# Another order and another choice of engines for the 4663 steps of a transformer block on one core

## The chip, the core and the metric

The kernel runs on one core of a Trainium2 chip. A core has five instruction streams that run side by side: TensorE (PE) for matrix products, VectorE (DVE), ScalarE (ACT) and GpSimd (POOL) for elementwise work, and SyncE (SP), which here issues every DMA. Each stream is executed strictly in order; streams wait for each other, and for DMAs, through semaphores. Products land in PSUM, which POOL cannot read; everything else lies in SBUF or in DRAM. The metric is the device time of one execution in microseconds; the number given is the median of several runs.

## The reference

One pre-norm transformer block over 2048 tokens with 512 channels, in float32:

```
h   = x + attention(layernorm(x)) @ wo         # 32 heads of 16, causal, window of 256
out = h + (sigmoid(n @ w_gate) * (n @ w_up)) @ w_down,   n = layernorm(h)     # F = 1376
```

Attention masks every key that is in the future or 256 or more positions back, takes a softmax over the rest and weighs the values with it.

## The kernel before

**Numbers in halves.** Apart from the product with v, every float32 operand of a product is split into a float16 high half and a float16 low half, and a product is three matmuls: high x high, high x low, low x high (`mm3`, the loop in `multiply`). Making the halves costs two elementwise steps: a copy or scaling to float16 (ACT or DVE: L355, L357, L954, L1024, L1104) and a subtraction (DVE or POOL: L362, or DVE alone where a scale is applied: L956, L1026).

**Stages.** First x is normalized (`do_ln`), and wq, wk, wv are loaded, scaled and split (`prep`). For each of 8 blocks of 256 tokens the kernel then makes q and k (`do_qk`), v (`do_v`), the scores once for their row maximum (`do_s`: PE L740, DVE L725), feeds the maxima back as extra rows of the queries by DMAs (`do_m`), makes the scores again, transposed (`do_st`: L794 to L805), takes their exponentials (ACT L770), zeroes the masked corners (POOL L778, L783), multiplies with v (`do_pv`: L831), transposes the result by a DMA and adds the halves (`do_o`: L861), divides by the sums (`do_wo`: L875), splits (L362), transposes (to `oT`) and multiplies with wo, adding x (L899).

The GLU stage works on pairs of 128-token tiles. `do_ln2` normalizes the pair, splits it (L1104, L362) and transposes it by a DMA; the buffer of halves, `hl2`, is one deep, so the second half of a pair's work on ACT waits for the first transposition. `do_pair` multiplies with the gate and up weights by a scheme of seven products in place of eight (P1 to P7, L1140); the sums between them are elementwise steps on DVE or ACT (`copied`, `added`). `gated` takes the sigmoid (ACT L1206) and the product of gate and up (L1210); `hidden` forms the sums S1 to S4 (L1224) and splits four rows (L355 or L357 for the high half, L362 for the low), each then transposed by a DMA (L1240). `do_down` multiplies with w_down (L1317, L1323), again by seven products, and adds to h (L1288, L1300). The weights are prepared beside the attention and at the start of the GLU stage: w_gate and w_up by `do_weights` (subtractions T1 to T4: L1045 and L362), w_down by `do_split` (subtractions D1 to D4: L362; halves L954, L956).

**What sets the order.** The kernel is written as 492 pieces, each one or more Python generators. A generator yields before a step with the engines that may take it, the events it needs and the ring buffers it takes. A list of numbers, `ORDER`, says which generator runs its next step and on which engine; `Planner.run` walks the list once and emits the instructions of each step. So the list fixes, for each of the five streams, which instructions it gets and in what order. One number holds three things:

```
self.now = self.roots[code >> 7]                # the piece of work
item = self.now[code >> 2 & 31]                 # its part
self.on = next(iter(costs)) if len(costs) == 1 else ENGINES[1 + (code & 3)]   # 0 DVE, 1 ACT, 2 POOL
```

Steps with a choice of engine call `alt(...)`: the copies `cp`, `hhi`, `hi`, `raw`, `v`, `qk` (ACT or DVE), the subtractions and sums `lo`, `lo2`, `less`, `less2`, `dless`, `hsum`, `hlo`, `gate`, `oadd`, `on`, `wlo` (POOL or DVE), the maxima `am`, `amax` (ACT or DVE). The costs written beside them were used by the search that made the list and play no part when the kernel runs; the position in the list is not a time, only an order.

Of the kernel before, what the change touches and what calls it, by code (L numbers as in the profile page):

```python
# [61 lines left out]
    3203, 3331, 771, 899, 1027, 1155, 7424, 2179, 2435, 7808, 7426, 1411, 7424, 641, 2051, 7810, 7424, 641, 1539, 7424, 1667, 7808, 641, 7427, 7808,  # L62
    3459, 7810, 1795, 641, 2307, 6658, 640, 7424, 3587, 643, 7811, 640, 2691, 3075, 641, 7808, 2947, 640, 641, 2819, 640, 641, 8323, 640, 641, 8323,
    640, 8323, 1280, 1281, 1921, 8323, 1921, 3715, 8195, 1281, 1280, 1920, 8323, 13056, 1921, 8323, 8323, 8323, 1280, 12672, 13058, 1283, 8321, 8195,
    8195, 1280, 8195, 3843, 12674, 8195, 2561, 8195, 1920, 7042, 8320, 8195, 8195, 1281, 1923, 8193, 1280, 8451, 2561, 2560, 8192, 1281, 1280, 1281,
    8579, 9219, 1280, 1281, 2561, 3971, 8451, 9219, 1280, 8451, 8835, 12672, 8579, 6018, 1920, 8835, 12673, 8451, 13056, 9219, 1921, 8451, 12672,
    8451, 4099, 1921, 8451, 18304, 8451, 8963, 8579, 1922, 8449, 8579, 8963, 2560, 8579, 1921, 8448, 8579, 8835, 6274, 8579, 1921, 13056, 8579, 8963,
    17920, 12675, 13058, 8577, 2563, 12673, 8576, 17922, 1920, 1921, 8707, 13059, 18306, 7683, 8707, 1920, 13057, 1920, 7683, 1921, 8067, 1920, 8067,
    1920, 7683, 17920, 49667, 8067, 23168, 17921, 4227, 8067, 17920, 8707, 7683, 50691, 8064, 7681, 51075, 2560, 9091, 17923, 18304, 13443, 8707,
    2561, 13443, 23552, 13443, 2561, 13443, 17921, 13443, 18304, 4355, 23554, 13443, 18304, 13443, 6402, 9091, 13443, 28416, 13571, 13441, 13571,  # L70
    6530, 9091, 13571, 10371, 10371, 13571, 10372, 10376, 6786, 13571, 13440, 13571, 13571, 13571, 10371, 10371, 10371, 13569, 10384, 23170, 13699,
    10388, 13699, 50688, 2562, 13699, 10380, 49665, 13699, 13568, 13699, 13699, 13699, 13699, 23168, 10371, 10371, 14467, 10371, 13697, 13827, 10392,
    10400, 13827, 4483, 9347, 10396, 13827, 9348, 14211, 13827, 13696, 9347, 9347, 9347, 13827, 14083, 9352, 13827, 9360, 10883, 14211, 9356, 13827,
    10884, 13827, 28800, 14211, 18307, 13825, 10883, 9347, 10883, 18305, 9364, 10888, 13824, 9347, 10883, 2561, 9368, 18691, 13955, 10892, 33664,
    18691, 2561, 14083, 9347, 18691, 23169, 18691, 14467, 9372, 9347, 18691, 10896, 23170, 13955, 18819, 9376, 9603, 18691, 14467, 9604, 10883, 10883,
    9603, 10900, 18691, 10904, 51203, 9608, 18691, 23552, 10883, 9603, 9603, 18689, 18819, 10908, 4611, 9616, 18819, 10883, 9612, 18819, 10912, 18819,
    18688, 18819, 18819, 13955, 9603, 9603, 18819, 9603, 50435, 2560, 2561, 18817, 18947, 51331, 18947, 9620, 9624, 14339, 18947, 9628, 51073, 18947,
    18816, 14083, 9603, 18947, 2561, 18947, 14339, 18947, 2562, 18947, 50179, 9632, 11139, 10115, 19075, 18945, 10116, 10115, 11140, 19075, 10120,
    13955, 2561, 6146, 11139, 11139, 19075, 11144, 11148, 19075, 2561, 18944, 11139, 7170, 10115, 19075, 10115, 11152, 19075, 10128, 19075, 14339,
    10124, 11139, 12931, 11156, 34048, 28418, 11139, 10115, 10115, 19075, 12931, 19073, 10136, 11160, 12931, 10132, 51201, 19072, 11139, 11139, 10115,  # L80
    12931, 11164, 11168, 10140, 10115, 13315, 12929, 10144, 50433, 12416, 11651, 11651, 11651, 13315, 11652, 11656, 12419, 11660, 11651, 13315, 11664,
    11907, 11907, 13315, 11908, 11912, 0, 11651, 11651, 11651, 18563, 13313, 11668, 11672, 12419, 11676, 51329, 11651, 11907, 11907, 11680, 23171,
    11916, 18563, 49411, 11920, 23169, 23552, 19203, 11907, 11907, 11907, 18563, 11928, 23554, 19203, 11924, 11932, 11907, 16387, 16387, 11936, 9475,
    9475, 18563, 33666, 16388, 9477, 9481, 16392, 16387, 28802, 16387, 18561, 9475, 16396, 16387, 9475, 6914, 9485, 12544, 16387, 9489, 23555, 16400,
    12547, 16404, 9475, 23553, 16387, 18179, 16408, 28416, 16387, 9497, 15619, 16412, 9475, 4739, 18179, 16416, 50177, 50051, 15620, 15619, 9731,
    24195, 9501, 12547, 15624, 15619, 15619, 24195, 9733, 15628, 28417, 15619, 9731, 15632, 9731, 24195, 19203, 9741, 15636, 15619, 24195, 9737,
    15640, 15619, 15619, 9731, 15644, 9731, 9745, 24195, 15648, 9753, 15363, 9750, 9731, 15364, 15363, 24195, 9757, 19331, 9506, 15368, 10243, 16899,
    15363, 24195, 10245, 16900, 9494, 10243, 10243, 15372, 9859, 16899, 10249, 16899, 9762, 24195, 10253, 38912, 50049, 15363, 10243, 28418, 10243,
    9859, 10257, 16908, 10265, 16904, 7298, 49409, 15376, 16899, 28800, 10243, 15363, 16912, 16899, 10269, 10499, 4867, 18179, 15380, 50819, 9857,
    16916, 10499, 10274, 15363, 18179, 19331, 10501, 15384, 10505, 9856, 10499, 15363, 18177, 16899, 14851, 10499, 15388, 10509, 24323, 28419, 10513,  # L90
    16920, 10499, 14852, 10518, 15363, 10499, 10521, 16899, 15392, 24323, 10262, 50563, 16924, 10525, 14851, 16899, 24323, 14856, 19331, 50817, 14851,
    11011, 16928, 10530, 24323, 19459, 11013, 14851, 14860, 24323, 39296, 11011, 10627, 14851, 19459, 11011, 14851, 10627, 11021, 28801, 49795, 14872,
    19459, 11017, 14864, 28802, 24193, 14868, 11011, 9987, 11011, 11025, 14851, 24192, 24323, 11033, 2562, 11011, 14876, 14851, 14595, 11037, 28803,
    11267, 14880, 24323, 14595, 11030, 14596, 11269, 11267, 14595, 10625, 14600, 11267, 24323, 34050, 11273, 14604, 14595, 14595, 11277, 11042, 14608,
    11267, 11281, 11267, 14612, 14595, 11289, 11267, 11286, 14616, 14595, 11395, 14595, 19587, 10624, 11293, 11779, 17155, 14620, 11781, 10755, 11779,
    11298, 14624, 11785, 11779, 17155, 24321, 17664, 17155, 11395, 17156, 11789, 17667, 49793, 24320, 17160, 11779, 17164, 17155, 24451, 11779, 11793,
    17168, 19843, 24451, 11801, 11779, 11798, 19844, 17155, 19843, 11805, 17172, 12035, 17155, 17667, 19848, 12037, 12035, 11810, 19843, 17176, 12041,
    12035, 17155, 19852, 12045, 19587, 12035, 17155, 17180, 12049, 12035, 19843, 11393, 17184, 12035, 12054, 19843, 19856, 12061, 19715, 19843, 19860,
    19843, 12057, 29443, 19715, 11392, 12163, 20867, 29443, 19864, 19715, 12066, 29443, 14723, 19587, 19843, 33664, 14723, 14725, 12163, 19868, 51843,
    33665, 19872, 4995, 14729, 20868, 20867, 50561, 14723, 20872, 20867, 14723, 14733, 29443, 20876, 20867, 14737, 20867, 29443, 20880, 14723, 12161,  # L100
    20884, 20867, 14742, 14723, 14749, 20867, 24067, 20892, 20867, 14753, 24067, 20888, 14979, 24067, 12160, 14981, 14758, 24067, 20896, 14979, 9986,
    16131, 24067, 44160, 14985, 14979, 14746, 16131, 11523, 29443, 14989, 14979, 16132, 16131, 29443, 16136, 14993, 14979, 16140, 16131, 16131, 15005,
    24067, 14998, 16144, 14979, 16148, 16131, 16131, 15009, 15491, 16152, 29443, 15002, 16156, 15493, 20099, 24067, 15014, 20100, 15491, 20099, 15491,
    10754, 20104, 20099, 16131, 24067, 16160, 20099, 12291, 15107, 15107, 24065, 29440, 20108, 17792, 15501, 20112, 17795, 15497, 29440, 51840, 20099,
    15105, 15491, 49539, 20116, 15491, 20099, 15505, 23939, 20120, 23939, 15517, 17795, 12288, 15491, 20099, 11520, 20611, 15521, 20611, 15747, 15514,
    20612, 23939, 49923, 15749, 20124, 15747, 15510, 23939, 20616, 15753, 20099, 15747, 20128, 20611, 20611, 15757, 15526, 15747, 20620, 23939, 15761,
    15104, 20611, 15747, 23939, 20624, 15773, 15747, 15770, 20611, 20628, 23939, 19203, 15777, 15766, 7552, 20611, 16259, 24064, 20611, 15875, 16259,
# [1392 lines left out]
```

## Time and profile before

| what | value |
| --- | --- |
| median of 3 runs | 767.21 us (766.03 to 768.69) |
| the profiled execution | span 769.3 us; the profile gives no other time for it |
| TensorE matmuls | 729.6 us busy, 95% |
| VectorE | 692.9 us, 90% |
| ScalarE | 436.9 us, 57% |
| GpSimd | 256.7 us, 33% |
| DMA, the queue of all transfers | 117.35 MB, 67.9% of 16 engines' span |

"Busy" is the union of an engine's instruction spans. A group row names line, engine, operation, output<-inputs, shapes and count, then the group's busy time in us, the mean of one in ns, and the idle time of the engine just before its instructions with what ended it. In a timeline row the first two numbers are start and length in us; a bracket at the end gives the idle time before the row and its releaser. Attention runs until about 460 us, with the first GLU products mixed in from 415 on; from there to the end it is the GLU stage.

### The profile page before, as it was taken

Reading aid. Unit: us, or ns where it says so; the run is one execution under the profiler, and the core shown is the slowest. Engines: PE = TensorE matmul, PEld = TensorE weight load, DVE = VectorE, ACT = ScalarE, POOL = GpSimd, SP = SyncE. Lnnn points to the kernel's source line nnn. Section 1 sums busy time; section 2 is a strip of 40 time slices with the busy share of each in tenths; the row PEclk is TensorE's granted clock in tenths of the full one; section 3 lists DMA queues with packets and bytes.
Section 4 is the critical chain, followed back from the end, with each engine's and each line's share of the span. In section 5 each row is a group of like instructions: output and inputs, shape, how many; then the busy total and the mean of one; then the engine's idle time right before and its main releaser. Section 6 shows DMA issues by size and latency. Waiting matters only on the chain.

```text
span 769.3 us, 19057 instructions
## 1 busy us (share of the span) xinstructions
PE 729.6 (95%) x7030; PEld 502.0 (65%) x7030; DVE 692.9 (90%) x2067; ACT 436.9 (57%) x774; POOL 256.7 (33%) x319
## 2 busy tenths in 40 slices
PE   4899999999999999999999898699999999999997
PEld 3586678777686687686666554367565666666476
DVE  8999999978899999999998579999998989989973
ACT  5755788878688888798877667653222111121210
POOL 3333445535545466554757442240000000000000
PEclk9999999999999999999999999899999999999999
DMA  8586593886747989569587879455375665736535
GB/s 300 156 221 168 142 180 80 152 198 144 165 95 172 205 211 182 166 156 245 150 162 180 211 187 274 117 119 105 79 136 95 117 131 106 150 66 109 96 83 155
DMA packets 210318, 118.57 MB, mean 154 GB/s; under 512 B 174576, under 2 KB 183792, under 8 KB 210224
## 3 DMA queue, kind: packets, MB, share of 16 engines
q1 hardware_dynamic: 210224, 117.35, 67.9%
q8 instruction: 55, 0.90, 0.5%
q14 instruction: 39, 0.32, 0.2%
HBM read 43.65 MB, written 19.40 MB: 82 GB/s over the span
## 4 chain that ended last, share of the span: by engine, by line
PE 75%; DVE 11%; DMA 5%; issue 5%; ACT 3%; SPq 0%; DVEq 0%; ACTq 0%
PE mmp L402 18%; PE sp L1140 14%; PE mmp L1317 11%; PE pvp L831 7%; PE sp L740 6%; PE stp L1140 6%; PE pvp L1140 3%; PE stp L805 2%; PE stp L795 2%; DVE junk L725 2%; PE stp L794 1%; PE mmp L1323 1%; PE stp L796 1%; DMA oT<-whl 1%; ACT pa L770 1%
## 5 line engine op out<-in xcount | busy, mean ns | idle before, releaser
L725 DVE CUSTOM_DVE_ANT_0 junk<-sp,mask 128x320 uint8<-128x320 f32 (+4 forms) x512 | 215.4, 465 | 16.6 <-PE sp L740 14.0
L770 ACT ACTIVATE pa<-stp,kappa 128x512 f32<-128x512 f32 (+1 forms) x256 | 157.3, 645 | 48.0 <-PE stp L796 44.5
L1140 PEld LDWEIGHTS <-x 128*128 128x128 f16 x1008 | 98.3, 98 | 94.6 <-issue 10.1
L740 PE MATMUL sp<-SK,SQ 96*128 96x256 f16 (+3 forms) x960 | 129.6, 233 | 6.3 <-DVE mq L725 3.1
L402 PE MATMUL mmp<-xT,W 128*128 128x256 f16 x768 | 114.3, 281 | 3.3 <-DVE sq L661 1.7
L740 PEld LDWEIGHTS <-SQ 96*128 96x128 f16 x960 | 80.5, 97 | 30.9 <-issue 12.8
L1140 PE MATMUL sp<-W,x 128*128 128x512 f16 (+1 forms) x420 | 90.1, 351 | 6.5 <-ACT SQ L355 5.8
L770 ACT ACTIVATE pb<-stp,kappa 128x512 f32<-128x512 f32 x128 | 84.6, 685 | 19.7 <-PE stp L805 15.9
L402 PEld LDWEIGHTS <-W 128*128 128x128 f16 x768 | 71.4, 100 | 16.1 <-DVE W L539 2.9
L778 POOL TENSOR_SCALAR_AFFINE_SELECT pa<-pa 128x1024 f32<-128x1024 f32 x56 | 62.9, 1127 | 53.9 <-ACT pa L770 50.3
L831 PE MATMUL pvp<-pa,VT 128*17 128x128 f32 (+1 forms) x1408 | 62.5, 307 | 0.0
L795 PE MATMUL stp<-SQ,SK 100*128 100x256 f16 x224 | 60.2, 272 | 0.0
L563 POOL TENSOR_TENSOR rs<-rs,nhalf 128x1 f32<-128x1 f32 x32 | 20.2, 634 | 118.2 <-DVE rs L560 105.0
L783 POOL TENSOR_SCALAR_AFFINE_SELECT pa<-pa 128x512 f32<-128x512 f32 x64 | 42.6, 669 | 45.3 <-ACT pa L770 45.0
L1206 ACT ACTIVATE SQ<-sp,cg 128x512 f32<-128x512 f32 (+1 forms) x22 | 14.0, 636 | 76.6 <-PE sp L1140 76.3
L796 PE MATMUL stp<-SQ,SK 100*128 100x128 f16 x256 | 55.5, 219 | 0.7 <-ACT pb L770 0.4
L783 POOL TENSOR_SCALAR_AFFINE_SELECT pb<-pb 128x512 f32<-128x512 f32 x64 | 42.0, 658 | 42.6 <-ACT pb L770 40.1
L402 PE MATMUL mmp<-WO,oT 128*128 128x512 f16 x192 | 51.4, 389 | 2.5 <-DMA oT<-whl 2.5
L831 PEld LDWEIGHTS pvp<-pa,VT 128*17 128x17 f32 x1408 | 37.8, 97 | 22.7 <-issue 2.7
L362 DVE TENSOR_TENSOR SQ<-SQ,SQ 128x512 f16<-128x512 f32 (+3 forms) x93 | 50.2, 555 | 1.9 <-ACT SQ L355 1.3
L794 PE MATMUL stp<-SQ,SK 100*128 100x128 f16 x224 | 49.5, 221 | 1.3 <-DMA SQ<-mt 0.3
L805 PE MATMUL stp<-SQ,SK 100*128 100x256 f16 x256 | 48.1, 272 | 2.5 <-ACT pa L770 2.1
(226 smaller groups left out, 1445.8 us busy)
## 6 DMA issues: line engine op xcount, KB each, us to landing
SQ<-sq SPq DMA_DIRECT2D x96, 128.0 KB
wr<-chunk SPq DMA_DIRECT2D x28, 256.0 KB
SK<-mem SPq DMA_DIRECT2D x16, 384.0 KB
chunk<-in_wd_dram SPq DMA_DIRECT2D x20, 256.0 KB
X<-in_x_dram SPq DMA_DIRECT2D x16, 256.0 KB
mem<-sk SPq DMA_DIRECT2D x8, 512.0 KB
out_dram<-X SPq DMA_DIRECT2D x16, 256.0 KB
W<-wr SPq DMA_DIRECT2D x7, 512.0 KB
```

What stands on the lines that cost most here:

```text
L402: PE.matmul(ps, a_of(a, k), b_of(b, k), start=(k == 0 and i == 0), stop=(k == n - 1 and i == 2))
L725: V.tensor_tensor_reduce(out=junk[:, c0:], in0=ps[:, c0:], in1=mask[:, c0:], scale=1.0, scalar=-3.0e38, op0=ALU.add, op1=ALU.max, accum_ou ...
L740: PE.matmul(ps[:, col:col + k1 - k0], q, SK[0:96, (2 * a + hf) % 5, 4 * (p % 2) + j, k0:k1], start=True, stop=True)
L770: S.activation(dst, a, AF.Exp, scale=kappa)
L778: G.affine_select(out=f, in_=f, pattern=[[0, 8], [-1, 128]], compare_op=ALU.is_gt, fill=0.0, base=0, channel_multiplier=1)
L783: G.affine_select(out=p, in_=p, pattern=[[0, 4], [1, 128]], compare_op=ALU.is_ge, fill=0.0, base=0, channel_multiplier=-1)
L795: PE.matmul(a[:, 128:384], ks(k0 + 1, g, j), qs(b, g, j, 0, 256), start=True, stop=True)
L796: PE.matmul(a[:, 384:512], ks(k0 + 3, g, j), qs(b, g, j, 128, 256), start=True, stop=True)
L805: PE.matmul(a[:, u, :], ks(k0 + 2, g, j + u), qs(b, g, j + u, 0, 256), start=True, stop=True)
L831: PE.matmul(ps[32 * j:32 * j + 17, u, q0:q1], VT[:, kt % 6, 8 * j + g, :], w[:, j, c:c + q1 - q0], start=first, stop=last, skip_group_chec ...
L1140: PE.matmul(ps, X2[p % 2][part][:, (a * COUNT[part] + at) * 2 + k, :], operand(c, j)[:, b, k, :], start=first and k == 0 and i == 0, stop= ...
L1317: PE.matmul(ps, hT[p, c, r][:, a, half * kinds[c] + i, :], W["d"][2 * c + i][:, b, j, :], start=fresh and c == 0 and i == 0 and n == 0, st ...
```

## The change

Only the list `ORDER` is replaced. The new one has 4663 entries like the old: every step of every generator is there once, so the matmuls, the transfers and the arithmetic are the same. What differs is the order within each stream and the engine of steps that have a choice. In words the change is described as: order and engine of all steps searched anew over the whole kernel, with transfers that land late by varying amounts and a shared port of VectorE and GpSimd.

```diff
 ORDER = [
-    3203, 3331, 771, 899, 1027, 1155, 7424, 2179, 2435, 7808, 7426, 1411, 7424, 641, 2051, 7810, 7424, 641, 1539, 7424, 1667, 7808, 641, 7427, 7808,
...
-    61591, 62224, 62211, 62211, 62211, 62211, 62228, 62211, 62231, 62211, 62211, 62211, 62232, 62235,
+    3203, 7427, 7427, 3331, 3587, 7811, 7811, 7427, 7043, 13059, 13059, 771, 7425, 1027, 899, 643, 1155, 643, 7811, 7424, 1539, 2179, 7808, 2051,
...
+    62211, 62146, 62211, 62211, 62147, 62227, 62211, 62211, 62211, 62211, 62211, 62211, 62231, 62231, 61591, 62211, 62235, 62235,
 ]
```

Two entries show how it reads. The gate product of pair 0, chunk 1 is entry 57500 in the old list (piece 449, part 7, engine 0: DVE) and 57502 in the new (engine 2: POOL). The sum S1 of the same pair is 57512 and becomes 57514. By kind, the steps that change from DVE to POOL are 48 sums S1 to S4, 21 gate products, 42 low halves of rows, the subtractions of `do_split`, `do_weights` and `do_ln2`, and 11 additions of `do_o`; from DVE to ACT go mostly the copies `cp` (30) and high halves `hhi` (39).

| engine | steps before | steps after | in the old mutual order |
| --- | --- | --- | --- |
| TensorE | 1729 | 1729 | 1081 |
| VectorE | 1424 | 1217 | 524 |
| ScalarE | 710 | 767 | 479 |
| GpSimd | 299 | 449 | 175 |
| SyncE (DMA) | 501 | 501 | 249 |

The last column is the largest number of steps that stand on the engine in both lists and in the same order.

438 rows, old and new, of the table ORDER are left out of this document.

## The prediction, made before the result

> **What bounds the kernel now.** I read the page first, then the busy time by stretch, then the instructions around each pause of TensorE, then the groups by shape.
>
> ```profile
> span 769.3 us, 19057 instructions
> PE 729.6 (95%) x7030; PEld 502.0 (65%) x7030; DVE 692.9 (90%) x2067; ACT 436.9 (57%) x774; POOL 256.7 (33%) x319
> ...
> DVE  8999999978899999999998579999998989989973
> ...
> POOL 3333445535545466554757442240000000000000
> ```
>
> TensorE (PE) and VectorE (DVE) are both near full, but these are averages over different stages. GpSimd (POOL) stops working after slice 23. The stretches, cut where the stages change:
>
> ```profile
> core 0: us, PE busy (x) PEld busy (x) DVE busy (x) ACT busy (x) POOL busy (x), PEclk, DMA share, GB/s
> 0.00:40.00 40.00, 26.87 (x176) 17.68 (x177) 35.45 (x84) 25.92 (x51) 13.22 (x28) 0.96 0.73 230
> 40.00:415.00 375.00, 365.61 (x4486) 272.69 (x4484) 351.62 (x1318) 293.85 (x517) 195.22 (x236) 1.00 0.75 168
> 415.00:460.00 45.00, 42.86 (x455) 24.07 (x454) 28.71 (x58) 31.56 (x52) 22.30 (x26) 1.00 0.79 193
> 460.00:505.00 45.00, 34.90 (x173) 17.09 (x172) 44.41 (x88) 31.36 (x58) 9.81 (x10) 0.89 0.80 202
> 505.00:760.00 255.00, 254.74 (x1708) 166.81 (x1708) 230.77 (x520) 54.26 (x99) 16.17 (x22) 1.00 0.56 107
> 760.00:769.00 9.00, 4.59 (x41) 3.63 (x38) 1.99 (x3) 0.00 (x0) 0.00 (x0) 0.99 0.41 148
> ```
>
> Read the first number after each length: PE is idle for 13.1, 9.4, 2.1, 10.1, 0.3 and 4.4 us, 39.4 in all. From 505 to 760, a third of the span, it does not pause. That "busy" is real there: six matmuls of 512 columns start 1.30 us before the next six, then 1.29, with nothing in between, and one wait of 0.6 us stands in the whole stretch.
>
> ```profile
> 639.94 1.46 PE L1140 MATMUL sp<-SK,x 128*128 128x512 f16 x6
> 641.24 1.46 PE L1140 MATMUL stp<-SK,x 128*128 128x512 f16 x6
> ```
>
> ```profile
> PE sp L1140 <- ACT SQ L355: 0.6, 1, 0.6
> ```
>
> So whatever the new lists do after 505, they can only lose there; a gain must come from before. The narrowest place is 460 to 505, where DVE works 44.41 of 45 us while PE rests for 10.1. PE's largest pauses from 415 on:
>
> ```profile
> 432.41 0.38 PE L805 MATMUL stp<-SQ,SK 100*128 100x256 f16 x2 [1.94 <-ACT pa L770]
> ...
> 464.07 4.36 PE L402 MATMUL mmp<-WO,oT 128*128 128x512 f16 x12 [2.14 <-DMA oT<-whl]
> ...
> 485.84 0.91 PE L1140 MATMUL stp<-W,x 128*128 128x352 f16 x5 [1.13 <-DVE W L1026]
> ...
> 495.61 1.92 PE L1140 MATMUL sp<-W,x 128*128 128x352 f16 x6 [5.77 <-ACT SQ L355]
> ```
>
> The last is the costliest. ScalarE's (ACT's) queue just before it, then POOL's and DVE's:
>
> ```profile
> 492.87 0.72 ACT L954 ACTIVATE WD<-chunk,sd 128x512 f16<-128x512 f32 x1 [2.25 <-POOL chunk L362]
> 494.57 0.63 ACT L355 ACTIVATE SQ<-SQ 128x512 f16<-128x512 f32 x1 [0.99 <-DVE SQ L1210]
> 495.11 0.45 ACT L355 ACTIVATE SQ<-sp 128x352 f32<-128x352 f32 x1
> ```
>
> ```profile
> 475.04 2.15 POOL L362 TENSOR_TENSOR chunk<-chunk 128x256 f32<-128x256 f32 x1 [6.04 <-DVE WD L956]
> ...
> 491.89 0.94 POOL L362 TENSOR_TENSOR chunk<-chunk 128x256 f32<-128x256 f32 x1 [6.48 <-DVE chunk L362]
> ```
>
> ```profile
> 491.34 0.41 DVE L362 TENSOR_TENSOR chunk<-chunk 128x256 f32<-128x256 f32 x1
> ...
> 493.85 1.29 DVE L1210 TENSOR_TENSOR SQ<-SQ 128x512 f32<-128x512 f32 x2
> ```
>
> PE waits for a PSUM copy (495.11) that is ready to run but stands in ACT's queue behind a half of a w_down piece (492.87). That half waits for a POOL subtraction, which waits for a DVE subtraction (491.34 + 0.41) inside a DVE queue without a gap. A full DVE reaches PE by way of two other queues.
>
> **The change part by part.** Nothing is added or removed: both lists hold the same 4663 steps, hence the same matmuls and transfers. I followed both lists through the planner's loop and counted, for each step, its engine and its place on that engine. In all 170 go from DVE to POOL and 20 back, 98 from DVE to ACT and 41 back. The prices:
>
> ```profile
> L362 DVE TENSOR_TENSOR chunk<-chunk 128x256 f32<-128x256 f32 x12 | 4.9, 413 | 0.0
> L362 POOL TENSOR_TENSOR chunk<-chunk 128x256 f32<-128x256 f32 x8 | 8.5, 1057 | 32.3 <-DVE chunk L362 17.2 <-DVE WD L956 11.5 <-ACT WD L954 2.3
> L1224 DVE TENSOR_TENSOR SQ<-SQ 128x256 f32<-128x256 f32 x62 | 26.7, 437 | 0.5
> L1224 POOL TENSOR_TENSOR SQ<-SQ 128x256 f32<-128x256 f32 x2 | 1.6, 784 | 2.9 <-DVE SQ L1224 2.9
> L362 DVE TENSOR_TENSOR SQ<-SQ,SQ 128x512 f16<-128x512 f32 x46 | 31.0, 683 | 0.9 <-ACT SQ L355 0.7
> L875 POOL TENSOR_TENSOR OS<-OS,rc 128x512 f32<-128x512 f32 x9 | 9.9, 1102 | 4.0 <-DVE rc L873 4.0
> L861 DVE TENSOR_TENSOR OS<-RT 128x272 f32<-128x272 f16 x17 | 8.5, 511 | 0.0
> L861 POOL TENSOR_TENSOR OS<-RT 128x272 f32<-128x272 f16 x15 | 11.4, 763 | 4.2 <-DVE whl L362 4.2
> L362 DVE TENSOR_TENSOR whl<-OS,whl 128x512 f16<-128x512 f32 x9 | 6.6, 735 | 0.0
> L362 DVE TENSOR_TENSOR X<-X 128x512 f32<-128x512 f32 x3 | 3.0, 986 | 0.0
> ```
>
> *460 to 505.* Of the steps that stand in this stretch now, 27 leave DVE for POOL: 8 subtractions of do_split, 3 of do_weights, 6 sums and 3 gates of the GLU, 5 low halves of rows, a normalization and a split of do_wo. One low half comes back, and 3 high halves come from ACT. DVE loses 8 x 0.413 + 11 x 0.437 (256 and 352 columns) + 8 x 0.683 (512 columns) = 13.6 us and gets back 0.683 + 3 x 0.437 = 2.0: its 44.4 become 32.8. POOL gets 11 x 1.057 + 8 x 0.784 + 8 x 1.102 = 26.7, less 1.1 for the one that leaves: its 9.8 become 35.4. PE is busy for 34.9. Three engines then stand near 35 where one stood at 44.4, so the ceiling of the gain is PE's idle 10.1. Against it: the subtractions D1, D3, D2, D4 of w_down now all run on POOL, in one queue with the sums, and 17 POOL steps stand from the sum S1 of the first pair to the last D4, on which a half in ACT's queue waits, with a PSUM copy of pair (0, 2) behind it. PE has over the same steps 5 groups of six 512-column matmuls (1.30 us each by the spacing above), 5 of six with 352 columns (352/512 of that) and 8 of three (half): 16.2 us. At 1.0 us per POOL step the copy comes about in time, at 1.2 us it is 17 x 1.2 - 16.2 = 4.2 us late. Ends: -10 and +5. I take -4, nearer to PE's idle row, since the ACT copy still stands behind such a half.
>
> *40 to 415.* 28 steps go from DVE to POOL (11 of L861, 5 splits of do_wo, 3 subtractions of do_weights, 2 normalizations, the rest small) and 12 come back (4 normalizations, 4 splits of do_ln, 2 splits of do_wo, 2 of L861). The large ones: 9 x 0.511 + 3 x 0.735 + 3 x 0.986 = 9.8 us off DVE, less 2 x 0.683 + 4 x 0.683 = 4.1 back; the small rest (8 steps near 0.43) gives 3.4: 9.1 net, of 351.6. Between DVE and ACT 21 go one way and 22 the other, taken as nothing. DVE is idle for 23.4 us here and so not the bound all the time; PE shows 9.4 idle. Ends: -9 (all of it reaches PE) and +4 (PE's local order changes too, only 1081 of its 1729 steps keep their mutual order, and nine of the old gaps of 0.4 us would make 4). I take -2, a quarter of the relief.
>
> *0 to 40.* 13 steps leave DVE, 8 come to it, at the same order of prices; PE's first work stays in place. Ends -2 and +1; -0.5.
>
> *The transfers.* Only 249 of the 501 DMA steps keep their mutual order on SyncE's (SP's) queue, so loads of the w_gate and w_up halves and the transpositions to oT, mt and x2 pass each other. What a late one costs now is seen twice above: 2.14 (oT), and 1.94 behind the second half of ln2, which ACT starts only when hl2's first transposition has landed:
>
> ```profile
> 423.87 6.67 DMA x<-hl
> ```
>
> In the new lists the first half (L1104) stands 3.3 us of PE work earlier, with the matmuls around it in the old order; the oT transposition of the same place has the same kind of neighbours. SP itself waits, head of the queue:
>
> ```profile
> SPq L752 <- DVE mq L725: 33.4, 9, 6.7
> ```
>
> and whatever is queued behind waits with it. Ends: -4 (both pauses gone) and +6.7 (one more such wait reaches PE whole). I take -1.
>
> *505 to 760.* 111 steps go to POOL, 68 to ACT, 15 come to DVE. At the cheap end, 0.437 each, DVE sheds 164 x 0.437 = 72 us: 230.8 become 159. Nothing to win under a PE without a pause; each row chain (gate, two sums, low half) gets longer by 0.42 + 2 x 0.35 + 0.42 = 1.5 us, which two buffers of pairs in flight cover. If that cover goes, the next matmul of a pair waits. Ends 0 and +10; +1.
>
> *End.* The last 38 PE steps are the same in both. The last low half goes to POOL (1.1 against 0.68); the transposition that PE now waits for is behind it: 0, ends -1 and +2.
>
> Sum against the profiled execution: 769.3 - 4 - 2 - 0.5 - 1 + 1 = 762.8. Its span is the only time that execution has, 2.1 above the median of the three timed runs (767.2); I carry that over: **761**.
>
> Here a rule speaks against the change. POOL's same subtraction took 2.15 us at 475.04 and 0.94 at 491.89, in a stretch where DVE never rests. The Trainium skill, SBUF — State Buffer, "Who interferes with whom", says that a DVE instruction with two SBUF inputs and a GpSimd instruction that reads SBUF exclude each other: the later one blocks in full. The trace agrees in kind, 1.2 us lost once. It makes the third rival below, which is priced from rows.
>
> **The rivals.** *POOL takes DVE's place (slower).* Between 460 and 505 POOL's mean rises from 1.0 toward 2.15 because DVE's two-input work alternates with it. From 45 / (27 + 10) = 1.2 us per instruction POOL needs more than the whole stretch; at 1.5 it needs 55, 10 us more than now, with ACT's halves and copies behind it: 769.3 + 10 - 3.5 (other terms but GLU) - 2.1 = about 774. For it: the 2.15 and the row's mean of 1.057. Against: 0.94 beside a full DVE, and DVE is emptier afterwards.
>
> *Nothing measurable.* The 4 of 460 to 505 are lost to POOL's queue and a moved transfer takes 2 more: 769.3 - 2 - 0.5 + 2 - 2.1 = 766.7. For it: three quarters of the changes lie after 505, where PE is the bound. Against: DVE's 44.4 of 45 is relieved for sure.
>
> *The port in the GLU stage (slower).* Were every POOL instruction there to block DVE for its length, 111 x 1.057 = 117 us come on DVE's 159: 276 of 255, and PE waits: 761 + 21 = 782. It decides only if more than (255 - 159) / 117 = four in five block. Unlikely.
>
> *All of it.* The 10 of PE's idle, the 9 of DVE's relief and the 4 of transfers come whole: 769.3 - 23 - 2.1 = 744.
>
> **How the numbers follow.** Forecast (757 to 764.8) 0.47, all of it 0.09, nothing 0.18, POOL in DVE's place 0.22, the port 0.04. About 0.3%, 2.3 us, can be told from no change. Faster 0.56, same 0.18, slower 0.26. The low end takes half of the way to "all of it", 749; the high end the POOL rival with a moved transfer, 777. The forecast's own range is 755 to 766.
>
> **What would show it.** Right: DVE near 33 to 36 and PE idle under 7 in the 45 us before PE's pauses end; POOL busy in every slice to the end; no wait on ACT L355 above 3 us at a 352-column matmul; still under 1 us of PE waits from there to the end. Wrong: PE waiting on POOL or on DVE behind L362 or L1224 in the last third; the POOL group of 128x256 above 1.2 us mean; a single DMA-ended PE wait above 4 us; PE idle before 415 above 25 us.

## The result and the profile after

The new list takes 778.00 us (median of 4 runs, 776.97 to 778.73), against 767.95 us (766.03 to 770.97) for the old one on the same chip: a ratio of 1.012, 95% interval 1.009 to 1.015. It is slower by about 10 us. The profiled execution of the new kernel is one of the timed runs: span 775.5 us, time 777.5. Time is thus span plus about 2, and the old kernel's profiled execution (span 769.3) would be at about 771, above its median; so the two profiles differ by 6.2 us where the medians differ by 10.

First the page of the new kernel: the totals and POOL's row of slices.

```profile
span 775.5 us, 19217 instructions
PE 726.4 (94%) x7030; PEld 499.5 (64%) x7030; DVE 648.0 (84%) x1857; ACT 466.0 (60%) x834; POOL 396.6 (51%) x472
...
POOL 3344455444555455555767687663353454434350
```

The move took place: DVE 692.9 to 648.0 us, POOL 256.7 to 396.6 and at work in every slice but the last. The stretches of the new kernel, with the columns of those shown before (busy time and number of PE, PE loads, DVE, ACT, POOL):

```profile
0.00:40.00 40.00, 26.63 (x192) 18.38 (x193) 34.15 (x84) 27.94 (x55) 13.33 (x28) 1.00 0.67 221
40.00:415.00 375.00, 362.95 (x4477) 269.93 (x4476) 355.26 (x1306) 297.41 (x522) 206.07 (x249) 1.00 0.73 175
415.00:460.00 45.00, 43.36 (x453) 23.91 (x451) 27.46 (x51) 30.04 (x50) 28.58 (x33) 1.00 0.82 190
460.00:505.00 45.00, 31.67 (x158) 15.78 (x159) 44.86 (x61) 26.46 (x50) 33.88 (x32) 0.89 0.61 148
505.00:760.00 255.00, 250.19 (x1652) 161.36 (x1651) 182.34 (x354) 84.19 (x159) 114.40 (x132) 1.00 0.55 105
```

From 460 to 505 DVE is as full as before (44.86 against 44.41 us), but with 61 instructions in place of 88: one takes 0.74 us on average where it took 0.50. PE does 158 matmuls there instead of 173, at the same granted clock of 0.89 in both kernels. The groups by shape in this stretch show it. The old kernel:

```profile
L1026 DVE SCALAR_TENSOR_TENSOR W<-WD,sg,W 128x352 f16<-128x352 f32 x9 | 5.6, 625 | 0.0
L362 DVE TENSOR_TENSOR SQ<-SQ,SQ 128x512 f16<-128x512 f32 x6 | 4.0, 680 | 0.0
L1045 DVE SCALAR_TENSOR_TENSOR WD<-WD,ratio 128x352 f32<-128x352 f32 x3 | 1.6, 546 | 0.0
L1163 DVE SCALAR_TENSOR_TENSOR SQ<-sp,SQ 128x512 f32<-128x512 f32 x2 | 1.4, 677 | 0.0
```

and the new one, with POOL's largest groups below:

```profile
L1026 DVE SCALAR_TENSOR_TENSOR W<-WD,sg,W 128x352 f16<-128x352 f32 x9 | 8.7, 970 | 0.0
L362 DVE TENSOR_TENSOR SQ<-SQ,SQ 128x512 f16<-128x512 f32 x6 | 6.6, 1106 | 0.1
L1045 DVE SCALAR_TENSOR_TENSOR WD<-WD,ratio 128x352 f32<-128x352 f32 x3 | 3.0, 1011 | 0.0
L1163 DVE SCALAR_TENSOR_TENSOR SQ<-sp,SQ 128x512 f32<-128x512 f32 x1 | 0.7, 678 | 0.0
...
L362 POOL TENSOR_TENSOR chunk<-chunk 128x256 f32<-128x256 f32 x13 | 13.6, 1053 | 4.0 <-DVE chunk L362 2.3 <-DVE WD L956 1.4
L1224 POOL TENSOR_TENSOR SQ<-SQ 128x256 f32<-128x256 f32 x6 | 5.6, 938 | 1.3 <-DVE SQ L1210 1.1
```

The same instructions with two inputs in SBUF take 1.5 to 1.9 times as long. L1163, which reads one input from PSUM (`sp`), keeps its 0.68 us; over the whole new kernel, 22 such rows of 128x512 with one input in PSUM (L1161 and L1163) lie by more than half of their length beside a POOL instruction, and none takes more than 0.69 us. The longer rows are those that stand beside POOL's. DVE of the new kernel, in order of time:

```profile
461.59 1.22 DVE L1045 SCALAR_TENSOR_TENSOR WD<-WD,ratio 128x352 f32<-128x352 f32 x1
462.73 1.54 DVE L362 TENSOR_TENSOR SQ<-SQ,SQ 128x512 f16<-128x512 f32 x1
464.20 0.34 DVE L873 RECIPROCAL rc<-OS 128x32 f32<-128x32 f32 x1
464.46 0.78 DVE L1026 SCALAR_TENSOR_TENSOR W<-WD,sg,W 128x352 f16<-128x352 f32 x1
465.16 1.75 DVE L875 TENSOR_TENSOR OS<-OS,rc 128x512 f32<-128x512 f32 x1
466.83 1.24 DVE L1045 SCALAR_TENSOR_TENSOR WD<-WD,ratio 128x352 f32<-128x352 f32 x1
468.00 0.68 DVE L1210 TENSOR_TENSOR SQ<-SQ 128x512 f32<-128x512 f32 x1
468.60 0.57 DVE L1026 SCALAR_TENSOR_TENSOR W<-WD,sg,W 128x352 f16<-128x352 f32 x1
469.10 1.21 DVE L362 TENSOR_TENSOR whl<-OS,whl 128x512 f16<-128x512 f32 x1
```

POOL of the new kernel over the same time:

```profile
460.99 1.44 POOL L362 TENSOR_TENSOR SQ<-SQ,SQ 128x512 f16<-128x512 f32 x1
462.39 1.34 POOL L875 TENSOR_TENSOR OS<-OS,rc 128x512 f32<-128x512 f32 x1
463.69 1.17 POOL L362 TENSOR_TENSOR chunk<-chunk 128x256 f32<-128x256 f32 x1
464.82 1.54 POOL L1210 TENSOR_TENSOR SQ<-SQ 128x512 f32<-128x512 f32 x1
466.32 1.37 POOL L362 TENSOR_TENSOR WD<-WD 128x352 f32<-128x352 f32 x1
468.82 0.93 POOL L1224 TENSOR_TENSOR SQ<-SQ 128x256 f32<-128x256 f32 x1 [1.13 <-DVE SQ L1210]
```

POOL works without a gap from 460.99 to 467.69, and every DVE instruction with two SBUF inputs that starts in that time is lengthened, L875 from 0.68 to 1.75. In the 1.13 us in which POOL rests, DVE's next two take 0.68 and 0.57, their lengths in the old kernel. PE pays at the end of this queue, for the low half `whl` of a tile. PE's waits in the new kernel from 415 to 545 us:

```profile
PE sp L1140 <- DVE SQ L1163: 9.5, 4, 4.3
PE mmp L609 <- DVE whl L362: 5.5, 1, 5.5
PE mmp L1323 <- DVE SQ L956: 1.9, 1, 1.9
PE mmp L402 <- DMA oT<-whl: 1.7, 1, 1.7
```

All but the last are ended by DVE. For sums over a stage I use two measures, both worked out from the instruction rows. The *extra* of an engine is the length of each of its instructions beyond the tenth percentile of the same line and shape in the two profiles. PE's *lost time* is a stretch less its matmuls at the usual spacing of their shape; it counts slow starts and a lower granted clock (0.89 in the stretch above) as well as waits. Rows of one engine overlap by some 0.07 us, so the lengths of DVE's rows add up to more than the stretch (47.2 us in the 42 of the table's first row). PE's lost time of one profile is good to about 1.5 us: from 420 to 540, five profiles that follow the old list up to 540 us give 17 to 20 us, three that follow the new one 24.5 to 26.3. The old kernel's profile is also the slowest of its kind up to 420 us.

| | old | new |
| --- | --- | --- |
| DVE, 458 to 500: without extra / extra (us) | 45.1 / 2.1 | 32.2 / 13.9 |
| POOL, 458 to 500: instructions, extra (us) | 8, 3.5 | 29, 7.9 |
| DVE, 545 to 760: extra (us) | 2.7 | 15.4 |
| PE's lost time up to 420 | 49.8 | 48.9 |
| PE's lost time from 420 to 540 | 18.2 | 24.8 |
| PE's lost time from 540 to 760 | 0.2 | 1.7 |

DVE was relieved of 12.9 us of work in the narrow stage and given 11.8 us of longer rows instead, 0.56 us for each of the 21 POOL instructions added.

### The profile page after: what moved, and what is told of

It reads as the page before. It is cut to its first block, busy times and chain, and to the rows that moved or that the text cites. A ratio compares the mean times of both kernels' runs of the same rounds, so it can differ in the third digit from the quotient of the medians.

```text
span 775.5 us, 19217 instructions
## 1 busy us (share of the span) xinstructions
PE 726.4 (94%) x7030; PEld 499.5 (64%) x7030; DVE 648.0 (84%) x1857; ACT 466.0 (60%) x834; POOL 396.6 (51%) x472
## 5 line engine op out<-in xcount | busy, mean ns | idle before, releaser
L725 DVE CUSTOM_DVE_ANT_0 junk<-sp,mask 128x320 uint8<-128x320 f32 (+4 forms) x512 | 214.5, 464 | 13.9 <-PE sp L740 11.7
L740 PE MATMUL sp<-SK,SQ 96*128 96x128 f16 (+3 forms) x960 | 128.0, 232 | 10.0 <-DVE mq L725 7.8
L402 PE MATMUL mmp<-xT,W 128*128 128x256 f16 x768 | 110.9, 275 | 2.4 <-ACT W L537 0.9
L402 PEld LDWEIGHTS <-W 128*128 128x128 f16 x768 | 69.7, 98 | 13.6 <-DVE W L539 2.1
L362 POOL TENSOR_TENSOR SQ<-SQ,SQ 128x512 f16<-128x512 f32 (+3 forms) x43 | 44.9, 1052 | 43.9 <-ACT SQ L355 24.4
L795 PE MATMUL stp<-SQ,SK 100*128 100x256 f16 x224 | 59.8, 270 | 0.0
L1224 POOL TENSOR_TENSOR SQ<-SQ 128x256 f32<-128x256 f32 (+1 forms) x50 | 36.1, 729 | 41.2 <-DVE SQ L1224 29.7
L796 PE MATMUL stp<-SQ,SK 100*128 100x128 f16 x256 | 55.4, 218 | 0.1
L355 ACT ACTIVATE SQ<-SQ 128x512 f16<-128x512 f32 (+3 forms) x54 | 27.3, 520 | 42.3 <-POOL SQ L1224 11.5
L355 ACT ACTIVATE SQ<-sp 128x512 f32<-128x512 f32 (+1 forms) x36 | 19.6, 543 | 51.7 <-PE sp L1140 48.5
L402 PE MATMUL mmp<-W,xT 128*128 128x512 f16 x192 | 49.9, 378 | 0.0
```

The source lines that it names most:

```text
L355: S.activation(out, x, AF.Copy, scale=scale)
L402: PE.matmul(ps, a_of(a, k), b_of(b, k), start=(k == 0 and i == 0), stop=(k == n - 1 and i == 2))
L725: V.tensor_tensor_reduce(out=junk[:, c0:], in0=ps[:, c0:], in1=mask[:, c0:], scale=1.0, scalar=-3.0e38, op0=ALU.add, op1=ALU.max, accum_ou ...
L740: PE.matmul(ps[:, col:col + k1 - k0], q, SK[0:96, (2 * a + hf) % 5, 4 * (p % 2) + j, k0:k1], start=True, stop=True)
L795: PE.matmul(a[:, 128:384], ks(k0 + 1, g, j), qs(b, g, j, 0, 256), start=True, stop=True)
L796: PE.matmul(a[:, 384:512], ks(k0 + 3, g, j), qs(b, g, j, 128, 256), start=True, stop=True)
```

## The experiments

In each run the kernel before is timed beside it, and differences are taken against that (medians 767.6 to 768.7). Only `ORDER` differs, except in the three with extra POOL instructions. In e1 to e4 the traces' line numbers are 26 lower than in the listing, in the three with extra instructions one higher. In the cuts of the edits below, the lines with a minus are those of the list from which the run starts.

**Engines or order, over the whole kernel.** In e1 and e2 one of the two is put back everywhere, in e3 and e4 only some POOL steps. The entries of pair 0, chunk 1 show how: its gate product in all four lists, with e4's example from pair 2.

```diff
 e1: the new order, all engines old
-57502, 57514
+57500, 57512
 e2: the old order, all engines new
-57500, 57512
+57502, 57514
 e3: the new list, 42 steps of about 458 to 540 us from POOL to DVE
-57502, 57514
+57500, 57512
 e4: the new list, 96 steps after about 540 us from POOL to DVE
-58930
+58928
```

> The new order of all steps, but every step with a choice on the engine that it had in the old list (170 POOL steps go back to DVE, 98 ACT steps back to DVE, the opposite moves are undone too). Theory A, the port: POOL instructions that read SBUF hold up DVE's two-input instructions between 460 and 540 us, and this takes away what the change lost; expected 766 to 771, DVE's mean at L1026 128x352 from 460 to 505 back from 970 ns to about 625. Rival B, the order: transfers and matmuls that stand elsewhere cost the 10 us; expected 776 to 780 with the pauses of TensorE after 460 as they are now. An order searched with other engines may fit the old engines badly; then the time is above 778 and the run speaks for neither.

> The old order of all steps, with every step with a choice on the engine of the new list. Theory A, the port: the loss comes with the engines; expected 774 to 782, DVE full from 460 to 505 with the mean at L1026 128x352 near 970 ns. Rival B, the order: expected 765 to 768, like before, since the order is the old one.

> The new list, with the 42 steps that went from DVE to POOL between about 458 and 540 us (17 subtractions of w_down, gates, sums, low halves) back on DVE; all else as in the new list. Theory A, the port in this stage: TensorE's idle time lost between 420 and 540 us (6.6 more than before) comes back for the larger part; expected 770 to 773, and DVE's mean at L362 128x512 in the stretch back near 700 ns from 1106. Rival B, the order: 777 to 780. Rival C, DVE is the bound of this stage and the relief was real: putting 42 steps back on a full DVE costs 42 x 0.5 = 21 us of DVE work and the time rises to 785 or more.

> The new list, with the 96 steps that went from DVE to POOL after about 540 us back on DVE; all else as in the new list. Theory A says that this late part is covered by TensorE's work: the cumulated idle time of TensorE after 540 grew by 1.7 us only, so expected 776 to 778. Rival, the port in the GLU stage: if POOL's instructions there held TensorE up, they would give back 5 us or more: 773 or less.

Measured: e1 807.05 us (ratio 1.050, 1.048 to 1.052), e2 783.84 (1.021, 1.018 to 1.023), e3 776.47 (1.010, 1.008 to 1.013), e4 780.80 (1.016, 1.013 to 1.018). Neither part alone is good, and e2 lies a little above the range that was expected of it. The e1 result says that the new order is cut to its own engines: with the old ones PE waits for DVE everywhere, also after 505 us, where PE of e1 is busy for 236 of 255 us:

```profile
505.00:760.00 255.00, 236.37 (x1509) 147.77 (x1508) 219.32 (x484) 58.78 (x108) 18.55 (x24) 0.99 0.55 106
```

e3 was the test of the port theory in its simple form (take POOL away, get the time back), and that form falls: 776.5 is little below 778.0, above that theory's range and just under its rival's. Nor did 42 steps more on DVE cost 21 us. The stretch of e3 and one of its groups:

```profile
460.00:505.00 45.00, 34.48 (x159) 16.67 (x160) 44.73 (x84) 25.32 (x47) 9.60 (x7) 0.85 0.58 143
```

```profile
L336 DVE TENSOR_TENSOR SQ<-SQ,SQ 128x512 f16<-128x512 f32 x8 | 5.5, 688 | 0.0
```

DVE's instructions have their old lengths again (688 against 1106 ns), there are 84 of them instead of 61, and DVE is exactly as full. So on the new order the moves to POOL are worth nearly nothing in either direction. e4 lies above both of its expectations. It says that behind the new order the moves of the last third rather help: without them the time is 2.8 us longer (the two intervals just touch), and PE's lost time from 540 to 760 us is 5.4 us instead of 1.7. With the old order in the last third they aren't needed: e7 below, with that part wholly old, takes 777.5.

**Which stage.** e5 to e8 cut the two lists at one place: a first part from one, then what is left in the order and on the engines of the other.

```diff
 e5: new list to entry 3375, then old (e6: the mirror)
 56579, 39043, 57347,
-39424, 39424, 39043, 48256,
+57356, 48256, 56195, 39425,
 e7: new list to entry 3773, then old (e8: the mirror)
 58371, 58910, 58755,
-59143, 58756, 58371, 58920,
+58307, 58372, 58755, 58756,
```

> The new list up to the end of the attention (its first 3376 steps, to about 458 us), then the 1287 steps that are left in the order and on the engines of the old list. Theory S, the stage: the loss is made by the list's part for 460 to 540 us; expected 766 to 769, since the attention alone gave TensorE 0.9 us. Rival T: the attention hands over with its transfers or buffers later and the loss shows only afterwards; expected 775 to 779.

> The mirror: the old list up to the end of the attention (3377 steps), then the 1286 that are left in the order and on the engines of the new list. Theory S, the stage: 777 to 780, TensorE's idle time between 420 and 540 us near the 24.8 of the new list (18.3 in the old). Rival T: 767 to 769.

> The new list up to about 540 us (3774 steps), then the 889 that are left as in the old list, which gives DVE back nearly all of the late work. Theory S: the loss is made before 540, so 776 to 778. Rival L: the late part of the new list is to blame (its pauses sum to 1.7 us only); then 768 to 771. If DVE is behind with its work at 540, the old list's fuller DVE does worse than the new list there: above 779.

> The mirror: the old list up to about 540 us (3768 steps), then the 895 that are left as in the new list, with POOL busy to the end (14 of them are put a few places later, where a ring buffer asks for it). Theory S: 766 to 769, TensorE without a pause after 540 although POOL works beside DVE. Rival L: 775 to 779.

Measured: e5 767.41 us (0.9994, 0.998 to 1.001), e6 782.96 (1.019, 1.015 to 1.022), e7 777.51 (1.012, 1.009 to 1.015), e8 769.06 (1.001, 0.999 to 1.003). Theory S holds: the attention and the last third of the new list are each as good as the old ones, and the 10 us are made between 458 and 540 us. (e5 isn't the sum of two good parts, though: up to 415 us its PE is behind, and it makes that up by 540; see the account of 40 to 415 us below.) PE's lost time from 420 to 540 goes with it: 16.2 and 17.2 us in e5 and e8, 24.5 in e7. e6 lies above its expectation, and its cause is a seam of my cutting: in the new list SP issues two loads of w_down before the cut, at 450.05 us, and ACT waits 2.5 us for them; behind the old attention they are issued after it (at 458.83 us in e10, below), and ACT of e6 stands still:

```profile
463.76 0.51 ACT L954 ACTIVATE WD<-chunk,sd 128x256 f16<-128x256 f32 x1 [6.72 <-DMA chunk<-in_wd_dram]
```

The same wait stands in e10 and e13 below. What it costs in time is nearer 5 us than 7: e6 differs from the new kernel and from e7 by 5.0 and 5.5 us.

**Engines and order within the stage.** All else is the old list; entries between about 458 and 540 us take the new engines (e9), the new order (e10), or both (e13).

```diff
 e9: 41 steps to POOL, 4 back, 10 between DVE and ACT
-57500, 57512
+57502, 57514
 e10: the 397 steps in the new order; e13: and on the new engines
 49027, 58041, 57347,
-58036, 58045, 58020, 56195,
+33795, 34179, 56067, 56579,
```

> The old list with its old order everywhere; only the steps that stand between about 458 and 540 us take the engines of the new list (41 from DVE to POOL, 4 back, 7 from ACT to DVE, 3 from DVE to ACT). Theory A, the port (POOL's reads of SBUF lengthen DVE's two-input instructions there, so that the engines alone make the loss): 774 to 780. Rival B, the order of the stage makes the loss: 766 to 770. Rival R, the relief of DVE is real when the order is good: 760 to 765.

> The old list with only the 397 steps between about 458 and 540 us in the new order, and every engine as in the old list. Theory A: the order costs nothing by itself, 767 to 770. Rival B: the order makes the loss, 775 to 780. Both: 771 to 774. The new list with 42 of its POOL steps back on DVE was 776.5, which leans to B.

> The old list with the 397 steps between about 458 and 540 us in the new order and on the new engines, all else old. The corner that was missing beside engines alone (775.1) and order alone (783.5). If the two losses add up: 788 to 792. If the new order needs the new engines (it was put together for them) and they pay for a part of it: 777 to 782, and DVE's instructions there are lengthened by some 18 us in sum, as in the new kernel. If the engines change nothing on the new order: 783 to 784.

Measured: e9 775.11 us (1.010, 1.006 to 1.014), e10 783.54 (1.020, 1.017 to 1.023), e13 781.97 (1.017, 1.014 to 1.020). e10 and e13 contain the seam; less some 5 to 7 us for it they are at about 776 to 778.5 and 775 to 777. Without a seam, the engines alone lose 6.7 us (e9), the order with DVE's work back on DVE 8.4 (e3), and both together 10, much less than the sum. e9 is the clean test of the engines, in the old order. Its stretch:

```profile
460.00:505.00 45.00, 30.79 (x154) 15.56 (x155) 39.74 (x56) 27.04 (x51) 31.35 (x32) 0.89 0.75 180
```

DVE's work without extra falls from 45.1 to 31.9 us between 458 and 500, and its extra rises from 2.1 to 9.6: some 5 us of room do come free (39.74 busy of 45), but PE waits all the same, most in these three places (its waits in e9 from 460 to 505):

```profile
PE sp L1140 <- DVE SQ L1163: 3.9, 1, 3.9
PE sp L1140 <- ACT SQ L355: 3.6, 1, 3.6
PE stp L1140 <- DVE W L1026: 3.0, 1, 3.0
```

PE's lost time from 420 to 540 rises from 18.2 to 25.2 us. DVE isn't full here, so its longer rows are not the whole account. Behind two of the three waits stands POOL's own queue: ACT waits for POOL, and what PE needs stands behind ACT's row.

```profile
480.49 0.63 ACT L355 ACTIVATE SQ<-SQ 128x512 f16<-128x512 f32 x1 [5.05 <-POOL SQ L1224]
492.42 0.72 ACT L954 ACTIVATE WD<-chunk,sd 128x512 f16<-128x512 f32 x1 [3.39 <-POOL chunk L362]
```

Behind the first, DVE waits 1.97 us for ACT, and L1026, for which PE waits 3.0 us, comes later in its queue. The same ACT wait was 1.50 in the old kernel. Behind the second comes the ACT copy of `sp` for which PE waits 3.6; this one isn't new, since in the old kernel PE waits 5.77 us at that copy. ACT waits for POOL for 9.4 us in all between 458 and 506 in e9, 4.3 in the old kernel and 0.6 in the new one. In the chain that ended last, from 455 to 545 us, POOL's rows hold 19.6 us in e9 and none in the old kernel, whose chain runs through DVE at this place. So on the old order POOL's own queue very likely carries a part of the loss. One of POOL's shorter 128x256 rows takes 0.73 us (at 477.11 in e9), where DVE's mean is 0.41. How much is POOL's queue and how much DVE's longer rows, no run separates.

**By number, or by queue.** e14 and e15 divide the 41 moves.

```diff
 e14: the 13 weight subtractions
-56592, 56596
+56594, 56598
 e15: the other 28
-57500, 57512
+57502, 57514
```

> The old list with only the 13 subtractions of the w_down and gate/up weights moved from DVE to POOL between about 458 and 540 us. Theory A, the loss goes by the number of POOL instructions beside DVE's two-input ones: a third of the 6.7 us that all 41 moves cost, so 769.5 to 772. Theory Q, POOL's queue: these subtractions stand ahead of ACT's halves and of the copies behind them, so they carry the whole loss: 773.5 to 777.

> The other part of the same 41 moves: the 28 sums, gates, low halves, combinations and the two steps of the last tile's normalization go to POOL, the 13 weight subtractions stay on DVE. Theory A: two thirds of the loss, 771.5 to 775. Theory Q: none of it, 767 to 770.

Measured: e14 770.47 us (1.004, 1.001 to 1.006), e15 771.35 (1.005, 1.002 to 1.007). Their +2.9 and +3.8 add up to the +6.7 of e9, and PE's lost time, +3.3 and +3.1, to its +7.0. So the subtractions don't carry the whole, and e15 lies a little under what theory A said of it. But adding up doesn't tell number from queue: ACT waits for POOL between 458 and 506 for 8.4 us in e14 and 9.3 in e15, and the chain that ended last has 3.4 and 13.0 us in POOL's rows. The subtractions' share for each move is larger (0.22 us against 0.14), which theory A didn't say and the intervals neither show nor exclude.

**The port by itself.** From 540 us on, extra POOL instructions stand beside the old list: subtractions that read SBUF (e11: four ahead of every sixth step, e16: two) or memsets that only write it (e12: six). Their results are used by nobody.

```diff
         for code in ORDER:
+            if step >= 3767 and step % 6 == 0: self.extra()
...
+        probe = identh[:].bitcast(F32)
+        plan.extra = lambda: [G.tensor_tensor(out=probe, in0=probe, in1=probe, op=ALU.subtract) for _ in range(4)]   # e11
+        plan.extra = lambda: [G.memset(probe, 0.0) for _ in range(6)]                                                # e12
+        plan.extra = lambda: [G.tensor_tensor(out=probe, in0=probe, in1=probe, op=ALU.subtract) for _ in range(2)]   # e16
```

> The old list as it is, and from about 540 us on, ahead of every sixth step, four extra POOL subtractions of 128x64 float32, SBUF to SBUF, in a tile that nothing else uses any more (114 times four): POOL is busy about half of the time beside DVE, and nothing waits for its results. Theory A, a POOL instruction that reads SBUF shuts out DVE's two-input instructions: DVE, busy 230.8 of 255 us there, gets some 50 to 100 us longer, its mean at L1224 128x256 rises from 437 ns to 600 or more, TensorE waits for it, and the time is 785 to 840. Rival: POOL beside DVE costs nothing, 767 to 770 and 437 ns.

> The same at the same places, but with six memsets of 128x64 float32 in place of the four subtractions: POOL is about as busy, and writes SBUF without reading it. If the reads are what shuts DVE out (theory A), the time is 766 to 771 and DVE's means stay (L1224 128x256 at 437 ns). If any POOL work does it, or the extra instructions themselves, it is as slow as the run with subtractions.

> As the kernel with extra POOL subtractions from 540 us on, with two of them at each place in place of four. With four, DVE's instructions grew from 508 to 535 ns, 12 us in sum, and POOL's queue held the row statistics back (DVE waited 21.5 us for them). If the queue was the cause of the 813 us: 768 to 772 here, with POOL near 90 of 220 us and no wait of DVE for the row statistics above 1 us. If DVE's longer instructions were: about half of the 45 us, 785 to 795.

Measured: e11 813.42 us (1.060, 1.056 to 1.064), e12 770.30 (1.004, 1.001 to 1.006), e16 769.63 (1.003, 1.000 to 1.005). The time of e11 fits theory A, and yet isn't its proof: DVE's mean at the 256-column sum rose to 454 ns only. What was late was POOL's own queue, in which the row statistics (L563 in the listing) stood. DVE's waits in e11:

```profile
DVE chunk L574 <- POOL rs L564: 21.5, 7, 6.6
```

With half as many (e16) the queue has room, this wait is gone and so are 43 of the 45 us. What the port costs is then read from DVE's groups after 540 us. With memsets (e12):

```profile
L363 DVE TENSOR_TENSOR SQ<-SQ,SQ 128x512 f16<-128x512 f32 x35 | 23.7, 684 | 0.9 <-ACT SQ L356 0.7
L1225 DVE TENSOR_TENSOR SQ<-SQ 128x256 f32<-128x256 f32 x47 | 19.9, 429 | 0.5
...
L1383 POOL MEMSET identh<- 128x64 f32 x876 | 143.7, 164 | 49.5
```

and with the fewer subtractions (e16):

```profile
L363 DVE TENSOR_TENSOR SQ<-SQ,SQ 128x512 f16<-128x512 f32 x35 | 24.8, 715 | 0.9 <-ACT SQ L356 0.7
L1225 DVE TENSOR_TENSOR SQ<-SQ 128x256 f32<-128x256 f32 x47 | 20.9, 450 | 0.5
...
L1383 POOL TENSOR_TENSOR identh<-identh 128x64 f32<-128x64 f32 x298 | 118.2, 397 | 22.4
```

144 us of POOL that only writes leave DVE's lengths as they were (its extra after 545 us is 3.3 us, 2.7 without them); 118 us of POOL that reads add 8.1 us of extra to DVE, and PE, with DVE at 207 of 220 us, hardly waits. The times are up by about 2 us in both. In e12 the interval excludes no change, so something costs time there that isn't known; e16 can't be told from no change. The Trainium skill, "SBUF — State Buffer", "Who interferes with whom", says of reads and writes: a DVE instruction with two SBUF inputs contends with a GpSimd instruction that reads SBUF, not with one that only writes it. The traces agree on all three sides: reads (e16), writes (e12) and the PSUM input of L1163, which stays at 0.68 us.

**Which part of the stage.** The first 20 us of matmuls in this stage have 73 steps of DVE and POOL among them in the new list, 50 in the old one. e17 puts only that part back to the old list, e18 keeps only that part new.

```diff
 e17: from entry 3376 on the old list for 20 us of matmuls, then new again
-39424, 39424, 39043, 48256
+57356, 48256, 56195, 39425
 e18: new list to entry 3532, then old
 57410, 56474, 57603,
-56735, 56730, 57411, 56363
+44291, 44291, 44291, 56733
```

> The new list, with only its first part of the stage (about 458 to 490 us) replaced: from step 3376 on the old order and engines for the next 20 us of matmuls, then the rest in the new order and on the new engines. Theory F, the loss is made where 73 steps of DVE and POOL stand ahead of matmuls that had 50 ahead of them: 768 to 771. Rival G, it is made after that: 775 to 778.

> The mirror: the new list up to about 490 us (its first 3533 steps), then the rest in the order and on the engines of the old list. Theory F: 775 to 778. Rival G: 767 to 770. If a part can be caught up, because the weight steps that came early are not to be done later: 770 to 774.

Measured: e17 776.25 us (1.008, 1.006 to 1.011), e18 775.98 (1.009, 1.006 to 1.013). Both theories fall: either half loses 7 to 8 us, nearly as much as both. In e18 PE pays in the first half (5.5 us for `whl` and 4.6 for L1163, as in the new kernel), in e17 in the second (12.7 us lost between 480 and 500, against 9.5 in the old one). A DVE that is full over the whole stage would make PE pay wherever it next needs DVE. That fits e17 (DVE 44.86 us busy of the 45 from 460 to 505), less so e18 (40.99), and is not shown.

No list of these beats the old one; e5 (767.41 against 768.55 beside it) can't be told from it. What stays open is why the new order, with its POOL work of this stage back on DVE (e3), still loses 8 us. That it stands as 73 steps ahead of matmuls that had 50 is a fact of the list; that this is the cause was tried (e17, e18) and not shown.

## Why the prediction was wrong

**460 to 505, predicted -4.** This step failed. Its counting was right: DVE's work fell by 12.9 us (11.6 predicted), POOL's busy time rose to 33.9 (35.4 predicted). Wrong was to set "44.4 become 32.8" as DVE's busy time and to call DVE "relieved for sure". The step priced a move as the instruction's own length off DVE and POOL's length onto POOL; what it left out is what POOL's instruction costs DVE while it runs, 0.56 us each here, as much as DVE was spared (0.41 to 0.68). DVE stayed at 44.86, where 33 to 36 had been named as the sign of being right; PE's idle time in this stretch is 13.3 us, where under 7 had been named. From 420 to 540 PE lost 6.6 us more, where 4 less for this term and 1 less for the transfers had been forecast. That DVE's longer rows set the time is shown for the new kernel as far as its PE waits on a DVE that is full; the engines' move alone (e9) probably loses its 6.7 us in part through POOL's own queue.

**The rival "POOL takes DVE's place", 774.** Its place, sign and near enough its price (+7) were right, and 778 lies a little above the range's end. Its mark was not: POOL's 128x256 subtraction came out at 1.053 us, under the 1.2 from which the rival was to decide. The two engines hold each other up, and I had looked for the damage in the length of POOL's rows only, because the one lengthened row that I had quoted (2.15 us) was POOL's. In the new kernel it stands mostly in DVE's rows. The ACT chain that it named is absent from the new kernel, where PE's waits end on DVE and ACT waits 0.6 us for POOL. On the old order it is there: in e9 it stands behind the wait of 3.6 us. So that chain is not what made the new list slow.

**What was not in any case.** That the new order loses about 8 us in this stage with DVE's work back on DVE (e3) was no step of the prediction: order was priced through transfers and gaps of 0.4 us alone. The cause of it is open.

**40 to 415 and 0 to 40, predicted -2.5.** e5 measures the new attention alone: -1.1 us by the medians, which the interval doesn't tell from nothing. But the trace gives the step of -2 the wrong sign. PE's idle time before 415, a mark of the prediction, came out at 25.4 us, above the 25 that were to show it wrong, and it was a good mark: it is 20.8 to 22.5 us in the eleven kept profiles with the old attention and 24.9 to 26.3 in the seven with the new one. The table's 49.8 and 48.9 don't show this, because that one profile of the old kernel lost the most there. So at 415 us the new attention is some 3 us behind. In e5 PE loses 16.2 us from 420 to 540, where the old list loses 17 to 20, and by then it is level. DVE's extra rose up to 415 as well, from 14.2 to 25.3 us, which the step had left out; that this is what PE's idle time comes from isn't shown.

**Transfers, predicted -1.** No wait of PE that a DMA ended exceeds 4 us. The pause behind `ln2` is gone from the rows, that for oT is 1.66 instead of 2.14. That could be the 1 us; no run measures it alone. The table of moved steps ahead of the prediction doesn't give the largest number for two of its engines: followed step by step, PE's is 1003 instead of 1081 and SyncE's 264 instead of 249. No term and no bound is worked out from them.

**505 to 760, predicted +1.** Right in size for the last third: from 540 on PE lost 1.7 us instead of 0.2. From 505 on, as the step was cut, PE's idle time rose by 4.5 us (0.3 to 4.8), because the waits of the narrow stage run on to 527 us. And e8 puts the whole of the new late part at 0.5 us, not to be told from nothing. The rival with the port in this stage, 782, falls: 97 POOL instructions more add 12.7 us of extra to a DVE that is busy for 150 of 220 us, and PE covers it.

## What to carry to other kernels

A move of elementwise work from DVE to POOL frees DVE only as far as DVE does something else than read two inputs from SBUF while POOL runs; price it by the length of the other engine's rows as well (0.56 us for each POOL instruction in this narrow stage, 0.13 in the last third), and by POOL's own queue, for which ACT waited 9.4 us in e9; and look at which share of DVE's queue in that very stage reads PSUM or a single input. Where an engine is full for a whole stage, a trace row names the place where PE pays, not always the cause: put the parts back one at a time, by stage first. And when two orders are cut together to test them, look for the loads that one of them had issued before the cut.

## What the runs showed of the hardware

Beside POOL, DVE's instructions with two SBUF inputs took 1.5 to 1.9 times their length as a group, at worst 1.75 us instead of 0.68, and those that read one input from PSUM stayed at 0.68 to 0.69 us. Who pays depends on the lengths: beside a dense DVE a POOL subtraction of 128x64 took 397 ns in the mean of e16, where half of those in e11 took 293 or 294, and added only 27 ns of extra to DVE for each (8.1 us over 298), while POOL's 128x256 to 128x512 in the narrow stage added 0.56 us to DVE and 0.21 to themselves: (7.9 - 3.5) / 21. Of 900 memsets on POOL (e12), 855 took 143 to 153 ns, the other 45 between 177 and 664, and DVE's lengths stayed as they were (684 and 429 ns in the groups above). One of POOL's shorter 128x256 rows took 0.73 us (e9), where DVE's mean for that shape was 0.41 to 0.44 (old kernel).
